# Token-order loads and DMA transposes for the last batch's q and k, in place of TensorE transposes

## The chip, the cores and the metric

The kernel runs on one core of one Trainium2 chip. The metric is the time of one execution on the device in microseconds (us). Most executions of a kernel agree within 0.3%. A profile's span is 1.7 to 2.1 us shorter than that time, so spans are compared with spans and times with times.

## The reference, cut to what matters

There are 4 batches, 8 heads, 768 tokens, head size 64, 512 channels. Attention uses a local window of 96 tokens and 8 global tokens with a distance bias. Its output goes through a gated mixing over tokens and then a matmul over channels.

```python
scores = scale * np.matmul(q, k.transpose(0, 1, 3, 2))      # + bias, mask, softmax -> a
x = np.matmul(a, v)                                         # heads side by side: 768 x 512
theta = x @ w_theta
zr, zi = x * np.cos(theta), x * np.sin(theta)
y = np.einsum('ts,bsd->btd', w_tok_r, zr) + np.einsum('ts,bsd->btd', w_tok_i, zi)
u = x + y
out = u + np.maximum(u @ w_ch, 0.0)
```

q and k are drawn with a factor of 0.1, so the scores are small beside the bias. The comparison with the reference doesn't see q and k well.

## The kernel before

While batch b is mixed, batch b+1 goes through attention, and q and k of batch b+2 are transposed for it (`prep`). So a "mixing stage" holds three kinds of work. The stage is the mixing of batch 1, with attention of batch 2 and, before the change, `prep` of batch 3.

```python
def load_qk(b, h0, n, which=(0, 1)):          # GpSimd DMA, 6 tokens x 64 = one run per head and partition
    ...
        nc.gpsimd.dma_start(out=qk[:, i_, h0:h0 + n]..., in_=(q, k)[i_][b, h0:h0 + n].rearrange("h (p t) d -> p h (t d)", p=T))

def prep(b, p):                               # one pair of heads
    ...                                       # VectorE: qkn <- qk, two copies
    for i_, dst in ((0, qT), (1, kT)):
        ps = ps_small([T, NT, T], BF)
        with behind("pe"):
            for t_ in range(NT):
                nc.tensor.transpose(ps[:, t_, :], qkn[:, t_, i_].rearrange("p h d -> p (h d)"), ident)
        ...
        if i_ == 0: nc.vector.tensor_copy(out=dst, in_=src)      # qT
        else:       nc.scalar.copy(out=dst, in_=src)             # kT
    kglob(b, p)

def kglob(b, p):                              # VectorE: kG <- kT, then the global tokens' columns over it
    ...
    nc.vector.tensor_copy(out=kG, in_=kT[:, T:(NT - 1) * T].rearrange("p (t n) -> p t n", t=NT - 2))
    nc.vector.tensor_copy(out=kG[:, :, 0:NG], in_=kT[:, None, 0:NG].to_broadcast([T, NT - 2, NG]))

def xtrans(b, p, ...):                        # xT <- x_sb, needed by theta
    if b: nc.sync.dma_start_transpose(...)
def utrans(b, tt):                            # uT <- u, needed by the channel matmul
    ...   nc.sync.dma_start_transpose(out=uT, in_=u)

def mix(b, tt, g): ...                        # TensorE: ps <- zri, w_tokT; then VectorE: u <- x_sb, ps

def load_behind(b, tile):                     # called for batch 3, once theta of batch 1 can start
    g = nc.gpsimd.tensor_copy(out=gate, in_=tile).ins
    with tc.issue_after(g):
        load_all_qk(b)
        load_all_v(b)
```

Outside a few hand-ordered parts, a scheduler decides in which order each engine's queue holds the instructions. `behind("pe")` and the like name an instruction that must come first in that queue. The whole kernel:

The softmax here doesn't subtract the row's maximum and nothing guards it: scores larger than these inputs give would overflow.

## Time and profile before

The time is 176.44 us (median of 3 runs, 176.21 to 176.53).

| what | value | view |
|---|---|---|
| TensorE busy | 92% of a span of 174.7 us | page, part 1 |
| chain of waits: TensorE, VectorE, DMA | 56%, 23%, 4% | page, part 4 |
| TensorE busy in the altered stage, 76 to 108 us | 31.3 of 32 us | stretches |
| xT by DMA, 66 to 130 us: issue to landing, median and longest | 2.8 and 7.3 us | tile view |
| batch 3's loads: issued; last (v) landed | 73.7 to 78.3 us; 96.1 us | GpSimd timeline, tile view |

From the page of before, parts 1, 2 (a digit is the busy share of a fortieth of the span, in tenths) and 4:

```profile
PE 160.6 (92%) x1505; PEld 86.4 (49%) x1530; DVE 133.9 (77%) x300; ACT 102.2 (58%) x128; POOL 26.3 (15%) x31
PE   6469878999999899999999999999999989999991
PE 56%; DVE 23%; ACT 13%; DMA 4%; issue 2%; DVEq 0%; ACTq 0%
```

TensorE (PE) is at 8 or 9 tenths in every slice from the seventh to the last but one.

The stretch table of before, a row for each 4 us of the stage (start:end, length, busy time and instructions of each engine, granted TensorE clock, DMA, GB/s):

```profile
core 0: us, PE busy (x) PEld busy (x) DVE busy (x) ACT busy (x) POOL busy (x), PEclk, DMA share, GB/s
80.00:84.00 4.00, 3.88 (x36) 1.80 (x36) 2.10 (x5) 3.72 (x5) 0.00 (x0) 1.00 1.23 220
84.00:88.00 4.00, 3.73 (x52) 2.09 (x53) 3.49 (x7) 3.38 (x4) 0.00 (x0) 1.00 1.46 243
...
100.00:104.00 4.00, 3.95 (x47) 2.51 (x46) 3.93 (x9) 0.87 (x2) 0.00 (x0) 1.00 0.58 140
...
108.00:112.00 4.00, 3.95 (x19) 1.81 (x19) 2.93 (x8) 1.70 (x2) 0.00 (x0) 1.00 0.34 95
```

There is next to no idle TensorE time here. (The DMA share can exceed 1; it serves only to compare stretches.)

The chain of waits of before at the end of the stage (start, duration, what). L233 are the transposes that the change removes, L388 the mixing, L368 the theta matmuls with which batch 2's own mixing stage begins. Of their first 16, six can run before the last xT has landed, ten need it (the trace has a record of nine):

```profile
104.39 0.67 PE ps L233 x12
105.06 0.88 PE ps L413 x4
105.95 0.87 PE ps L233 x12
106.81 1.73 PE ps L388 x8
108.54 1.29 PE pb L368 x6
...
109.89 2.11 PE pb L368 x9
```

Twelve transposes cost 0.67 to 0.87 us of TensorE and lie on the chain. Theta of batch 2 gives two marks: its first matmul (108.38 us in TensorE's timeline) and the first that needs the last xT (109.89).

VectorE (DVE) in before, at the start of the stage:

```profile
77.42 1.91 DVE L377 TENSOR_TENSOR zri<-x_sb,cs 128x512 bf16<-128x512 bf16 x5
79.24 0.68 DVE L419 SCALAR_TENSOR_TENSOR o_sb<-ps,u 128x512 f32<-128x512 f32 x1
79.84 1.09 DVE L377 TENSOR_TENSOR zri<-x_sb,cs 128x512 bf16<-128x512 bf16 x3
```

The last three zri products, which every token tile of the mixing needs, are done by 80.9 us, and nothing stands in front of them.

### The profile page before, as it was taken

How to read it: one execution, taken by the hardware profiler on the slowest of the kernel's cores; microseconds unless marked ns; L12 is line 12 of the kernel's file. 1: busy time of each engine (PE TensorE's matmuls, PEld its weight loads, DVE VectorE, ACT ScalarE, POOL GpSimd, SP SyncE). 2: the span in 40 equal slices, each digit the busy share in tenths (PEclk: the TensorE clock that was granted, in tenths of full speed). 3: DMA queues.
4: the chain of work that ended last, by engine and by line, in shares of the span. 5: the costliest groups of instructions: out<-in, count | busy, mean ns of one | idle time of the engine just before them, and what ended most of it. 6: DMA issues, size and time to landing. Idle time of an engine off the chain costs nothing.

```text
span 174.7 us, 3707 instructions
## 1 busy us (share of the span) xinstructions
PE 160.6 (92%) x1505; PEld 86.4 (49%) x1530; DVE 133.9 (77%) x300; ACT 102.2 (58%) x128; POOL 26.3 (15%) x31
## 2 busy tenths in 40 slices
PE   6469878999999899999999999999999989999991
PEld 1245555456746566544455565443554634444440
DVE  7678965778999999996779999796866847723443
ACT  2479676999497694499854813779447408500010
POOL 8983355004000000190000000000000000000000
PEclk9999999999999999999999999999999999999999
DMA  5999999999999972479999955133145371414335
GB/s 157 183 192 182 206 208 208 204 205 165 166 204 167 159 116 45 109 90 216 244 148 103 168 135 135 34 121 90 21 87 134 90 168 27 172 31 101 114 90 180
DMA packets 58225, 24.36 MB, mean 139 GB/s; under 512 B 44256, under 2 KB 55264, under 8 KB 58208
## 3 DMA queue, kind: packets, MB, share of 16 engines
q0 software_dynamic: 35216, 12.45, 70.5%
q1 hardware_dynamic: 22576, 11.15, 28.8%
q10 hardware_dynamic: 416, 0.52, 0.9%
q8 instruction: 12, 0.20, 0.5%
q14 instruction: 5, 0.04, 0.1%
HBM read 25.69 MB, written 6.29 MB: 183 GB/s over the span
## 4 chain that ended last, share of the span: by engine, by line
PE 56%; DVE 23%; ACT 13%; DMA 4%; issue 2%; DVEq 0%; ACTq 0%
PE ps L388 25%; PE ps L413 10%; PE pb L368 7%; DVE x_sb L341 4%; PE pb L274 4%; PE pb L331 3%; ACT e L281 3%; PE ps L368 3%; ACT etab L133 3%; ACT cs L374 3%; DVE qT L238 2%; DVE e L291 2%; DMA qk<-in_k_dram 2%; DVE kG L208 2%; PE ps L233 2%
## 5 line engine op out<-in xcount | busy, mean ns | idle before, releaser
L388 PE MATMUL ps<-zri,w_tokT 128*128 128x512 bf16 x271 | 67.6, 379 | 1.2 <-issue 0.5
L281 ACT ACTIVATE e<-pb 128x1024 bf16<-128x1024 f32 (+1 forms) x48 | 43.5, 958 | 21.1 <-PE pb L274 21.0
L388 PEld LDWEIGHTS <-w_tokT 128*128 128x128 bf16 x288 | 25.9, 98 | 27.6 <-DVE w_tokT L160 0.6
L393 DVE TENSOR_TENSOR u<-x_sb,ps 128x512 bf16<-128x512 bf16 x24 | 16.4, 682 | 14.0 <-PE ps L388 14.0
L413 PE MATMUL ps<-w_ch_bf,uT 128*128 128x512 bf16 x94 | 23.7, 379 | 0.3 <-DVE u L393 0.2
L377 DVE TENSOR_TENSOR zri<-x_sb,cs 128x512 bf16<-128x512 bf16 x48 | 17.9, 418 | 7.9 <-ACT cs L374 7.6
L419 DVE SCALAR_TENSOR_TENSOR o_sb<-ps,u 128x512 f32<-128x512 f32 (+1 forms) x25 | 16.5, 662 | 3.1 <-PE ps L413 3.1
L274 PE MATMUL pb<-qT,kT 64*128 64x128 bf16 x224 | 15.6, 219 | 1.4 <-DVE qT L202 0.3
L291 DVE TENSOR_TENSOR e<-e,etab 128x1024 bf16<-128x1024 bf16 (+1 forms) x24 | 14.7, 616 | 2.5 <-ACT e L281 2.5
L274 PEld LDWEIGHTS <-kT 64*128 64x128 bf16 x224 | 9.1, 94 | 14.5 <-issue 12.5
L374 ACT ACTIVATE cs<-pb,halfpi 128x1024 bf16<-128x1024 f32 x8 | 8.9, 1115 | 11.5 <-PE pb L368 11.5
L240 ACT COPY kT<-ps 128x768 bf16<-128x768 bf16 x12 | 9.6, 798 | 10.3 <-PE ps L233 10.3
L368 PE MATMUL pb<-w_theta_bf,xT 128*128 128x512 bf16 x62 | 14.9, 379 | 0.6 <-DMA xT<-x_sb 0.5
L407 ACT COPY uT<-ps 128x512 bf16<-128x512 bf16 x7 | 4.1, 587 | 18.6 <-PE ps L406 18.6
L368 PEld LDWEIGHTS <-xT 128*128 128x128 bf16 x96 | 9.2, 98 | 11.1 <-DMA xT<-x_sb 1.0
L331 PEld LDWEIGHTS <-e 128*128 128x128 bf16 x352 | 12.6, 97 | 3.3 <-issue 1.6
L413 PEld LDWEIGHTS <-uT 128*128 128x128 bf16 x96 | 8.9, 98 | 10.0 <-ACT uT L407 0.3
L274 PE MATMUL pb<-qT,kG 64*128 64x128 bf16 x128 | 11.7, 217 | 1.5 <-DVE kG L209 1.4
L341 DVE TENSOR_TENSOR x_sb<-pb,rec 128x768 bf16<-128x768 f32 x12 | 11.4, 948 | 0.2
L79 POOL DMA_DIRECT2D vn<-in_v_dram x5 | 9.6, 1912 | 12.2 <-DVE vn L68 10.6
L238 DVE COPY qT<-ps 128x768 bf16<-128x768 bf16 x12 | 11.4, 947 | 0.0
L233 PEld LDWEIGHTS <-qkn 128*128 128x128 bf16 x144 | 9.0, 97 | 4.4 <-DVE qkn L218 1.4
(72 smaller groups left out, 200.9 us busy)
## 6 DMA issues: line engine op xcount, KB each, us to landing
out_dram<-o_sb SPq DMA_DIRECT2D x23, 256.0 KB, 2.2
qk<-in_q_dram POOLq DMA_DIRECT2D x3, 768.0 KB, 17.4
qk<-in_k_dram POOLq DMA_DIRECT2D x3, 768.0 KB, 19.3
vn<-in_v_dram POOLq DMA_DIRECT2D x3, 768.0 KB, 22.0
w_nat<-in_moe_w_tok_r_dram POOLq DMA_DIRECT2D x3, 384.0 KB, 14.0
w_nat<-in_moe_w_tok_i_dram POOLq DMA_DIRECT2D x3, 384.0 KB, 15.2
vn<-in_v_dram POOLq DMA_DIRECT2D x2, 384.0 KB, 8.8
qk<-in_q_dram POOLq DMA_DIRECT2D x3, 192.0 KB, 6.7
```

Source lines behind the costliest of these rows:

```text
L238: nc.vector.tensor_copy(out=dst, in_=src)
L274: nc.tensor.matmul(pb[:, hh, o:o + T], lhsT=lhsT, rhs=qT[R, (own, nxt)[part]], start=bool(b), stop=bool(b) or (jt == NT - 1 or (j == 1 and ...
L281: ins = nc.scalar.activation(e_c, pb[:, :, 0:n], AF.Exp, scale=scale).ins
L291: nc.vector.tensor_mul(e_c, e_c, tab[:, :, s0:s0 + n // T].rearrange("p a s n -> p a (s n)"))
L331: nc.tensor.matmul(o, lhsT=l_, rhs=r_, start=(i_ == 0), stop=(i_ == len(mms) - 1))
L341: nc.vector.tensor_mul(xv, po4[:, :, :, 0:D], rec.to_broadcast([T, n, NT, D]))
L368: nc.tensor.matmul(pb[j_] if last else pb[:, j_, :], lhsT=xT[:, dc, st(j_)], rhs=w_theta_bf[:, dc, :], start=(dc == 0), stop=(dc == NC - 1))
L377: nc.vector.tensor_mul(zri[b][:, i_, 2 * c + j_, :].rearrange("p (g d) -> p g d", g=NP), xb[:, :, 2 * c + j_, :], cs[:, i_, j_].rearrange( ...
L388: anchor["pe"] = nc.tensor.matmul(ps, lhsT=w_tokT[wi][:, st, tt * T:(tt + 1) * T], rhs=zri[b][:, wi, st, :], start=(st == 0 and wi == 0), ...
L393: anchor["dve"] = nc.vector.tensor_add(u_sb[b, tt].rearrange("p (g d) -> p g d", g=NP), x_sb[b][:, :, tt, :], ps.rearrange("p (g d) -> p g ...
L413: nc.tensor.matmul(ps_c, lhsT=uT[:, dc, :], rhs=w_ch_bf[:, dc, :], start=(dc == 0), stop=(dc == NC - 1))
L419: nc.vector.scalar_tensor_tensor(o_sb[:, cols], in0=ps_c[:, cols], scalar=0.0, in1=u[:, cols], op0=ALU.max, op1=ALU.add)
```

## The change

The intent is to relieve TensorE, the bounding engine. q and k of batch 3 are loaded in token order, one DMA per head and tensor (16 of them, with rows of 256 B), straight into the layout that a DMA transpose can take. SyncE issues eight DMA transposes to make qT and kT: pairs 0 and 1 in the mixing of batch 1, pairs 2 and 3 at the boundary to the next stage. That removes 48 transposes from TensorE, 8 qkn and 4 qT copies from VectorE, and 4 kT copies from ScalarE.

```diff
+    def load_qk_tokens(b):
+        qk = loads[b][0]
+        for h in range(H):
+            for i_ in range(2):
+                pair = qk[:, i_, h // 2 * 2:h // 2 * 2 + 2].rearrange("p h t d -> p (h t d)")
+                nc.gpsimd.dma_start(
+                    out=pair.rearrange("p (t h d) -> p t h d", t=NT, h=2)[:, :, h % 2],
+                    in_=(q, k)[i_][b, h].rearrange("(t p) d -> p t d", p=T))
...
+    def prep_dma(b, p):
+        qk = loads[b][0]
+        qkT[(b, p)] = [None, None, None]
+        for i_ in (1, 0):
+            to = qkT[(b, p)][i_] = att.tile([T, S], BF, name=("qT", "kT")[i_], bufs=6)
+            nc.sync.dma_start_transpose(
+                out=to.rearrange("p (t s) -> p t s", t=NT),
+                in_=qk[:, i_, 2 * p:2 * p + 2].rearrange("p h t d -> p (h t d)"))
...
         with tc.issue_after(g):
-            load_all_qk(b)
+            alloc_qk(b)
+            load_qk_tokens(b)
             load_all_v(b)
...
+        if b == B - 1:
+            add(0, kglob, b, 0)
...
+            if b == B - 1 and i_ in (0, 2, 6):
+                add(0, kglob, b, (1, 2, 0, 3)[i_ // 2])
...
-        ahead = [lambda p=p: prep(b + 2, p) for p in range(NP)] if b + 2 < B else []
+        ahead = [[lambda p=p: prep(2, p) for p in range(NP)], [lambda p=p: prep_dma(3, p) for p in range(2)],
+                 [], []][b]
         order = th[:4] + rest[:2] + th[4:] + rest[2:] if b else []
+        if b == 2:
+            order[:0] = [lambda p=p: prep_dma(3, p) for p in range(2, NP)]
```

The text of the change puts two pairs at the boundary and the kG copies in the next stage. The order that the scheduler built does neither: all eight transposes and all eight kG copies of batch 3 stand in SyncE's and VectorE's queues within the mixing of batch 1.

## The prediction

> **What bounds it now.** TensorE. The page has it busy 92% of 174.7 us. The chain of waits is 56% TensorE, led by the mixing matmuls (25%). In the stage that the change alters (mixing of batch 1 with attention of batch 2, about 73 to 109 us) the stretch table has TensorE busy 1.83 to 2.00 of every 2 us; VectorE is nearly as full from 94 to 109.
>
> **Removed.** 48 TensorE transposes: in the chain a group of 12 covers 0.67 us (one 0.87), so about 2.9 us of TensorE, all in that stage, nearly all critical. VectorE loses 8 qkn copies (0.34 us) and 4 qT copies (0.95), 6.5 us; ScalarE 4 kT copies (0.80), 3.2 us. If nothing else happened: 173.6 us.
>
> **Added.** 16 token-order loads of 768 rows of 256 B in place of 2. GpSimd issue took 0.72 us at 256 rows, 0.88 at 1024: about 0.85 each, 14 us, from 73.7 to 88. Movement: in the DMA stretches qk rows went at about 204 GB/s written, v (256 B rows) at about 155. The Trainium skill, "DMA: Bandwidth & Descriptors", Specifications, puts line rate at 512 B and up (this trace agrees). q and k then need 10 us rather than 7.7: issue paces them. v should land near 98 us, before its use at 109. Eight DMA transposes in SyncE's queue cost 1.2 us of issue and 2.8 us to landing (as the xT ones; 7.3 in contention).
>
> **Moved, and this costs.** In the built order the scheduler puts all eight kG copies of batch 3 early in VectorE's queue: the first ahead of the last three zri products of batch 1, the second pair before the first u. They wait for DMA-made kT. The same page (Anatomy of one DMA) says the issuing sequencer holds a semaphore wait: SyncE's eight transposes stand in order with outputs and uT.
> Estimate: the fourth load is issued near 77 and lands near 80; qT then kT of pair 0 issue at 79.5 and 80.7; kT lands 83.5 to 84.5. VectorE reaches that kG at 79.3: 4 to 5 us idle. The zri products held back finish at 86; TensorE's mixing of token tile 0 needs them at 82.5: a stall of about 3.5 us, where there was next to none. Pair 1's kG (kT about 87) delays VectorE a little; e products reach values(2,0) at about 90 against 87. Later kG break even. uT of batch 1 goes out at 88 rather than 84, needed at about 96: no stall.
>
> **Sum.** -2.9 + 3.5 + about 0.3 of secondary waits: +0.9 us. Predicted 177.3 us, range 174.6 to 181.0. Faster by over 2%: 0.05; within 2%: 0.78; slower by over 2%: 0.17.
>
> **What would show it.** Waits: a new line of VectorE kG waiting for DMA kT, longest 4 to 5 us, at 79 to 84; TensorE mixing waiting for zri, 3 to 4 us, at 82 to 86. From 90 us on TensorE without long gaps, theta of batch 2 starting at 108 to 110. GpSimd issues of 0.8 to 1.0 us. The stages after it unchanged within 0.5 us.
>
> **What would make it wrong.** kT of pair 0 landing by 81 (loads landing within 2.5 us): no stall, about 174. Or loads at 1.2 us of issue each and transposes slowed to 5 to 7 us by the load traffic: stalls at each of the four kG waits, uT late, 180 or more.

## The result, and the profile after

| kernel | median, us | lowest to highest | runs |
|---|---|---|---|
| before | 176.49 | 176.21 to 177.92 | 4 |
| after | 192.82 | 192.63 to 192.99 | 4 |

The ratio is 1.0907 (95% interval 1.0847 to 1.0967): the change makes the kernel 9% slower. A ratio here is the mean time of one kernel's runs over that of the other's of the same rounds, so it is not quite the ratio of the medians. Executions over 1.5% slower than the fastest of the same kernel are left out of the means. The prediction, 177.3 us and at most 181.0, was wrong.

From the page of after, parts 1, 2 and 4:

```profile
PE 165.8 (87%) x1457; PEld 86.0 (45%) x1482; DVE 128.4 (67%) x288; ACT 99.4 (52%) x124; POOL 38.0 (20%) x45
PE   5889979999999999923966669999999998999992
PEclk9999999999999999985578979999999999999999
DMA 32%; PE 32%; DVE 20%; POOL 8%; issue 3%; ACT 2%; SPq 1%; DVEq 0%; POOLq 0%
```

TensorE lost 48 instructions and yet is busy 5.2 us longer. There is a hole in its row at slices 18 to 24, which is 81 to 115 us, and in the same place the granted clock falls, to half at the lowest. The chain of waits, which DMA led for 4%, is now 32% DMA. Outside that stretch the row looks as before.

The stretch table of after:

```profile
80.00:84.00 4.00, 2.48 (x25) 1.08 (x24) 0.00 (x0) 3.37 (x4) 4.00 (x6) 1.00 2.24 126
84.00:88.00 4.00, 0.00 (x0) 0.00 (x0) 0.50 (x2) 0.00 (x0) 3.11 (x4) 0.57 2.05 175
...
100.00:104.00 4.00, 2.74 (x16) 0.93 (x14) 2.44 (x6) 1.02 (x1) 0.00 (x0) 0.80 2.01 136
...
108.00:112.00 4.00, 0.95 (x17) 0.51 (x17) 3.93 (x9) 1.03 (x2) 0.00 (x0) 0.98 0.46 91
```

From 84 to 88 us TensorE, ScalarE and almost all of VectorE stand still. Only GpSimd works: it issues loads. DMA is busier than in before, for longer.

VectorE's timeline of after. The bracket gives the idle time before an instruction and what ended it; L217 is the kG copy, L395 the zri products:

```profile
77.09 1.96 DVE L395 TENSOR_TENSOR zri<-x_sb,cs 128x512 bf16<-128x512 bf16 x5
87.50 0.29 DVE L217 COPY kG<-kT 128x512 bf16<-128x512 bf16 x1 [8.45 <-DMA kT<-qk]
...
88.31 1.08 DVE L395 TENSOR_TENSOR zri<-x_sb,cs 128x512 bf16<-128x512 bf16 x3
...
94.91 0.29 DVE L217 COPY kG<-kT 128x512 bf16<-128x512 bf16 x1 [4.63 <-DMA kT<-qk]
...
101.50 0.29 DVE L217 COPY kG<-kT 128x512 bf16<-128x512 bf16 x1 [3.23 <-DMA kT<-qk]
...
107.85 0.29 DVE L217 COPY kG<-kT 128x512 bf16<-128x512 bf16 x1 [3.06 <-DMA kT<-qk]
```

All four kG copies wait, not the first alone. The three zri products that ran at 79.84 us in before now run at 88.31, behind the first kG.

The waits of after, 70 to 145 us (engine and line, what for: us in total, times, longest), then the landing line of the kT transposes:

```profile
DVE kG L217 <- DMA kT<-qk: 19.4, 4, 8.4
PE ps L406 <- DVE zri L395: 6.6, 1, 6.6
```

```profile
DMA to landing us min/median/max: 7.2/8.8/9.9
```

Four pieces of the chain of waits of after:

```profile
79.67 6.45 DMA qk<-in_k_dram
...
86.26 8.62 DMA kT<-qk
...
98.75 9.07 DMA kT<-qk
...
125.90 2.33 PE pb L386 x10
```

The two kT transposes on the chain take 8.62 and 9.07 us from issue to landing. Ahead of the first stands the load of k of pair 1, itself 6.45 us from issue to landing. Theta of batch 2 starts at 124.08 us, 15.7 later than in before, waits 0.37 us for the last xT, and goes on at 125.90, 16.0 later. That is nearly all of the loss (the spans differ by 191.0 - 174.7 = 16.3 us).

The two in-order queues also held each other. From SyncE's timeline of after:

```profile
91.49 1.27 SPq L259 DMA_TRANSPOSE kT<-qk  x1
96.03 1.19 SPq L420 DMA_TRANSPOSE uT<-u  x1
...
98.75 3.48 SPq L259 DMA_TRANSPOSE kT<-qk  x1
```

uT could go out only at 96.03, because its u stood behind the second kG in VectorE's queue (94.91) and so behind the second kT. The fourth kT stood behind that uT in SyncE's queue; its load had landed by 96.1. It was issued at 98.75, and the fourth kG waited for it.

**The clock.** The span grew by 16.3 us; TensorE's busy time grew by 5.2 of it, its idle time by 11.1. Of the 5.2 us, 2.0 lie before 76 us, mostly at the kernel's start, where the change does nothing. From 76 us to the start of theta of batch 2 busy time grew by 2.9 us (34.7 against 31.8) and idle time by 12.6. Since about 2.9 us of transposes went from there, the same work took about 5.8 us longer (an estimate: 2.9 + 2.9). The group of mixing matmuls, over the whole span, shows most of it:

```profile
L388 PE MATMUL ps<-zri,w_tokT 128*128 128x512 bf16 x271 | 67.6, 379 | 1.2 <-issue 0.5
```

```profile
L406 PE MATMUL ps<-zri,w_tokT 128*128 128x512 bf16 x271 | 72.2, 401 | 8.1 <-DVE zri L395 6.6
```

The first line is of before, the second of after: the same number of matmuls (271 records in both), 4.6 us more. One-microsecond stretches of after show when the clock changes:

```profile
84.00:85.00 1.00, 0.00 (x0) 0.00 (x0) 0.00 (x0) 0.00 (x0) 1.00 (x2) 0.77 1.61 176
94.00:95.00 1.00, 1.00 (x5) 0.18 (x5) 0.10 (x1) 1.00 (x2) 0.00 (x0) 0.61 0.97 229
111.00:112.00 1.00, 0.66 (x10) 0.40 (x11) 1.00 (x3) 0.23 (x1) 0.00 (x0) 0.92 0.47 94
115.00:116.00 1.00, 1.00 (x5) 0.27 (x3) 0.69 (x1) 0.00 (x0) 0.00 (x0) 0.87 0.00 0
```

A mean of 0.77 in a stretch that starts at 1.0 and ends at 0.5 puts the change at 84.54 us. In the same way the others come to 94.78 (up), 111.84 (down) and 115.26 (up). The distances are 10.24, 17.06 and 3.42 us. (Between the second and the third there is one more dip, from 98.2 to 101.6 us, also 3.4 long.) The Trainium skill, "TensorE: Matmul & The Clock Gate", Part 1, says that the gate judges a free-running window of 3413 ns and halves the clock after an idle one. This trace agrees closely on the length: the distances are 3, 5 and 1 times 3.413. It does not bear out that the window has to be idle (see the end). In its windows at half clock TensorE is busy for 11.95 us in all, so half of that, 6.0 us, is an estimate of what the clock cost, close to the 5.8 above. So an idle gap here could cost twice, in itself and in half-speed work after it, and the second cost came in units of 3.4 us.

### The profile page after: what moved, and what is told of

Same layout as the page of the kernel before. It is cut to its first block, busy times and chain, and to the rows that moved or that the text cites. A ratio compares the mean times of both kernels' runs of the same rounds, so it can differ in the third digit from the quotient of the medians.

```text
span 191.0 us, 3630 instructions
## 1 busy us (share of the span) xinstructions
PE 165.8 (87%) x1457; PEld 86.0 (45%) x1482; DVE 128.4 (67%) x288; ACT 99.4 (52%) x124; POOL 38.0 (20%) x45
## 4 chain that ended last, share of the span: by engine, by line
DMA 32%; PE 32%; DVE 20%; POOL 8%; issue 3%; ACT 2%; SPq 1%; DVEq 0%; POOLq 0%
PE ps L406 18%; DMA qk<-in_k_dram 14%; DMA kT<-qk 9%; DMA w_nat<-in_moe_w_tok_r_dram 7%; PE ps L431 6%; DVE qT L247 4%; POOL qk L82 3%; DMA xT<-x_sb 3%; DVE e L309 3%; PE pb L386 2%; DVE x_sb L359 2%; PE pb L349 2%; POOL qk L73 2%; DVE qkn L227 2%; PE pb L292 2%
## 5 line engine op out<-in xcount | busy, mean ns | idle before, releaser
L406 PE MATMUL ps<-zri,w_tokT 128*128 128x512 bf16 x271 | 72.2, 401 | 8.1 <-DVE zri L395 6.6
L406 PEld LDWEIGHTS <-w_tokT 128*128 128x128 bf16 x288 | 27.2, 102 | 38.7 <-issue 13.4
L395 DVE TENSOR_TENSOR zri<-x_sb,cs 128x512 bf16<-128x512 bf16 x48 | 17.9, 418 | 8.5 <-ACT cs L392 8.1
L292 PE MATMUL pb<-qT,kT 64*128 64x128 bf16 x224 | 16.7, 228 | 5.5 <-DVE x_sb L359 4.6
L217 DVE COPY kG<-kT 128x512 bf16<-128x512 bf16 x16 | 5.0, 314 | 20.0 <-DMA kT<-qk 19.4
L392 ACT ACTIVATE cs<-pb,halfpi 128x1024 bf16<-128x1024 f32 x8 | 8.9, 1115 | 15.7 <-PE pb L386 15.7
L292 PE MATMUL pb<-qT,kG 64*128 64x128 bf16 x128 | 12.4, 225 | 0.2 <-DVE kG L218 0.2
L88 POOL DMA_DIRECT2D vn<-in_v_dram x5 | 9.6, 1919 | 12.6 <-DVE vn L68 10.2
L349 PE MATMUL pb<-vn,e 128*128 128x65 bf16 x168 | 9.9, 193 | 1.4 <-DVE e L309 1.0
L312 DVE TENSOR_TENSOR e<-e,etab 128x1024 bf16<-128x1024 bf16 x12 | 8.2, 684 | 3.5 <-ACT e L299 3.5
```

The costliest lines, as they stand in the source:

```text
L88: nc.gpsimd.dma_start(out=vn[:, h0:h0 + n, :, 0:D].rearrange("p h t d -> p (h t) d"), in_=v[b, h0:h0 + n].rearrange("h (t p) d -> p (h t) ...
L292: nc.tensor.matmul(pb[:, hh, o:o + T], lhsT=lhsT, rhs=qT[R, (own, nxt)[part]], start=bool(b), stop=bool(b) or (jt == NT - 1 or (j == 1 and ...
L349: nc.tensor.matmul(o, lhsT=l_, rhs=r_, start=(i_ == 0), stop=(i_ == len(mms) - 1))
L395: nc.vector.tensor_mul(zri[b][:, i_, 2 * c + j_, :].rearrange("p (g d) -> p g d", g=NP), xb[:, :, 2 * c + j_, :], cs[:, i_, j_].rearrange( ...
L406: anchor["pe"] = nc.tensor.matmul(ps, lhsT=w_tokT[wi][:, st, tt * T:(tt + 1) * T], rhs=zri[b][:, wi, st, :], start=(st == 0 and wi == 0), ...
```

## The experiments

Medians are beside the median of before in the same rounds. "Before" had 176.4 to 176.7 us in all of them. In the quoted expectations, theory A says that the waits of the kG copies in VectorE's queue are the loss, and its rivals say that the loss sits in the DMA traffic or in SyncE's order. Edits are against the changed kernel unless said otherwise.

| run | what | median, us | ratio to before (95%) |
|---|---|---|---|
| after | the change | 192.82 | 1.0907 (1.0847 to 1.0967) |
| e1 | kG copies late in VectorE's queue | 187.11 | 1.061 (1.0565 to 1.0656) |
| e2 | e1, 8 loads with rows of 1536 B (wrong) | 184.81 | one run |
| e3 | token-order loads, TensorE transposes | 177.93 | 1.0075 (1.0042 to 1.0108) |
| e4 | e1, DMA transposes behind uT in SyncE's queue | 182.65 | 1.0339 (1.0303 to 1.0375) |
| e6 | e4, all pairs at the boundary, kG on GpSimd | 176.14 | 1.0011 (0.9951 to 1.0072) |
| e7 | the change, loads issued at 35.7 to 70.0 us | 183.07 | 1.0358 (1.0317 to 1.0398) |
| e8 | e7 and e6 together | 182.40 | 1.0347 (1.0316 to 1.0379) |
| e9 | e6, v of batch 3 later, in halves | 177.21 | 1.0055 (1.0016 to 1.0095) |
| e10 | the change without its 16 loads (wrong) | 175.54 | 0.9953 (0.9925 to 0.998) |
| e11 | e6 without the 16 loads (wrong) | 175.33 | 0.9935 (0.9914 to 0.9957) |
| e12 | e6 for pairs 2 and 3 alone | 177.13 | 1.0039 (1.0017 to 1.006) |

### e1: the kG copies behind the mixing of batch 1

```diff
-        nc.vector.tensor_copy(out=kG, in_=kT[:, T:(NT - 1) * T]...)
+        with behind("dve") if b == B - 1 else nullcontext():      # behind the last u of batch 1
+            nc.vector.tensor_copy(out=kG, in_=kT[:, T:(NT - 1) * T]...)
```

> Only the eight kG copies of batch 3 move in VectorE's queue, from early in the mixing of batch 1 to behind the last u of batch 1; SyncE's order is unchanged. Theory A (the whole loss is VectorE held in order by kG copies waiting for kT): the 19.4 us of kG waits go, TensorE's 6.6 us wait for zri goes, about 174 to 175 us. Theory B (transposes and loads share the DMA engines, and SyncE's queue holds uT and xT behind eight transposes that wait for loads): the kG waits go, but chan of batch 1 now waits for uT, first uT landing near 100 us when TensorE wants it near 93; 180 to 185 us. Theory C (the loads alone slow everything): 188 or more.

It took 187.11 us (186.71 to 187.87), 5.7 less than the change. The waits of VectorE for kT are gone, and two others have come in their place. The waits of e1:

```profile
PEld L432 <- DMA uT<-u: 11.2, 2, 8.5
DVE o_sb L438 <- PE ps L432: 13.7, 8, 8.6
```

The channel matmul waits for uT. SyncE issues uT of the first token tile at 93.36 us (84.18 in before), because five of the transposes, issued from 79.41 to 91.02 us, stand in front of it in SyncE's queue; then it needs 7.74 us to land. So the kG waits were 5.7 us of a loss of 16.3, and theory A falls as the whole cause.

### e2: fewer and longer rows

```diff
-        for h in range(H):
-            for i_ in range(2):
-                ...                                   # 768 rows of 256 B
+        for p in range(NP):
+            load_qk(b, 2 * p, 2)                      # rows of 1536 B, one pair of heads
```

On top of e1. The tokens come out in another order, which is wrong.

> As e1_kg_late, but the 16 loads of 256 B rows are replaced by 8 loads of one pair each in rows of 1536 B: same bytes, a sixth of the packets; the result is wrong on purpose, because the tokens come in another order. If the 256 B packets are what slows the transposes (theory B1), kT and qT land 3 to 5 us after their issue in place of 6.0 to 9.9, and the time falls by 3 us or more against e1_kg_late. If any load traffic does it, or the transposes' own 768 packets (theory B2), they still take 6 us or more and the time is within 2 us of e1_kg_late.

One run took 184.81 us, 2.3 less than e1, between what the two sides expected. The landing line of kT tells more than the time does:

```profile
DMA to landing us min/median/max: 5.6/10.1/10.9
```

With rows of q and k six times as long the transposes land no sooner than in e1 (7.3, 8.4 and 9.4 us). Short rows of q and k are not needed for the slow landing. Whether short rows matter at all stays open: v, with rows of 256 B, was issued at 79.86 us and landed 24.2 us later, so it was in flight beside all eight transposes. The uT wait stays too, at 9.0 us.

### e3: the loads alone

```diff
+    def prep_tok(b, p):                               # as prep, but from the token-order tile: no qkn copies
+        ...
+                    nc.tensor.transpose(ps[:, t_, :], src[:, t_ * T:(t_ + 1) * T], ident)
...
-        ahead = [..., [lambda p=p: prep_dma(3, p) for p in range(2)], [], []][b]
+        ahead = [..., [lambda p=p: prep_tok(3, p) for p in range(NP)], [], []][b]
```

> Token-order loads kept, the DMA transposes undone: TensorE transposes straight from the loaded tiles (no qkn copies), at the places of the kernel before. If the transposes and their place in the queues make the loss, 175 to 177.5 us. If the 12288 small packets of the loads alone make it (theory C), 182 or more, with uT landing at 8 us or more.

It took 177.93 us (three runs from 177.83 to 178.00; a fourth, of 181.1, is a slow one and left out of the ratio): 1.4 us over before, a little above what was expected. Single uT and xT transposes took up to 10.2 and 10.6 us to land, at medians of 2.9 and 3.0. The loads without the DMA transposes of q and k therefore cost little, but the 2.7 us of VectorE's qkn copies that this version saves (8 of 0.34 us) don't show in the time either.

### e4: the transposes behind uT in SyncE's queue

```diff
+            with behind("sp"):                        # behind the last uT of batch 1 issued so far
                 nc.sync.dma_start_transpose(out=to..., in_=qk[:, i_, 2 * p:2 * p + 2]...)
...
-            nc.sync.dma_start_transpose(out=uT, in_=u)
+            anchor["sp"] = nc.sync.dma_start_transpose(out=uT, in_=u).ins
```

On top of e1.

> As e1_kg_late, and the eight DMA transposes are put in SyncE's queue behind the uT transposes traced before them, so that none of them waits for a load with uT behind it. Theory A: same as e1_kg_late. Theory B: uT of batch 1 lands in time as in the kernel before, no long TensorE gap in the mixing, 173 to 175.5 us: the 2.9 us of TensorE transposes are then saved.

It took 182.65 us (182.00 to 182.95), 4.5 less than e1 and far more than expected. Two pieces of its chain of waits:

```profile
90.56 9.00 DMA uT<-u
...
110.62 2.80 DMA xT<-x_sb
```

The first uT is now issued in time, at 83.93 us, and its matmuls run no later than in before. The second, in the lines above, lands 9.00 us after its issue: it is itself a DMA transpose and meets the same loads; TensorE waits 1.55 us for it. The last two xT are issued late, at 107.96 and 110.62 us, behind the transposes of q and k; theta of batch 2 waits 3.48 and 1.37 us for them. Moving the transposes in SyncE's order was worth 4.5 us, and what TensorE still waits for is DMA.

### e6: all pairs at the boundary, kG on GpSimd

```diff
# against e4
-        with behind("dve") if b == B - 1 else nullcontext(): ...
+        eng = nc.gpsimd if b == B - 1 else nc.vector
+        eng.tensor_copy(out=kG, ...)
...
-        ahead = [..., [lambda p=p: prep_dma(3, p) for p in range(2)], [], []][b]
+        ahead = [..., [], [], []][b]
-            order[:0] = [lambda p=p: prep_dma(3, p) for p in range(2, NP)]
+            order[:0] = [lambda p=p: prep_dma(3, p) for p in range(NP)]
```

> All eight DMA transposes of batch 3 stand in SyncE's queue behind the last uT of batch 1, so after the loads have landed (about 106 us) and after every xT and uT of the mixing; the kG copies of batch 3 run on GpSimd, idle by then, so neither VectorE nor SyncE holds anything behind a load. Theory B (place in the queues and the transposes' sharing of the DMA engines with the loads make the loss): kT and qT land in about 3 us each, uT and xT no slower than in e3_loads_only, 174 to 175.5 us, that is e3_loads_only less the 2.9 us of TensorE transposes. If DMA transposes cost as such (theory D: they slow whatever runs beside them), the loss moves to theta and attention of the next batch and the time stays at 178 or more.

It took 176.14 us, 176.39 for before: the same. Three runs lie between 176.08 and 176.18; the fourth, the profiled one, took 178.31. The transposes of q and k now land in 2.8 us (median of kT; longest 4.5), after the loads. The mixing of batch 1 ends earlier: its last eight matmuls start at 103.25 us, against 106.65 in before, 3.4 us sooner. Then, in the chain of waits of the profiled run:

```profile
101.51 6.27 DMA xT<-x_sb
...
107.83 4.92 PE pb L388 x14
```

The last xT but one takes 6.27 us to land, while v of batch 3 is still under way (it lands 18.4 us after issue, near 106). Theta of batch 2 starts at 104.98 us but could continue only at 107.83, after 2.25 us of idle TensorE, and in this run then at half clock. In this run the gain of 3.4 us was turned into a wait for a transpose that the change doesn't even touch. The other three runs are 2.2 us faster, two of them with a granted clock of 1.000 throughout, so they can't have lost all of this; they have no trace that shows how much of the wait they share.

### e7 and e8: loading early

```diff
-    def load_qk_tokens(b): ...                        # into the qk buffer, at 73 us
+    def load_qk_tokens(b, p):
+        pairs[p] = moe.tile([T, 2, S], BF, name="w_nat", bufs=6)      # a buffer whose weights are used up
...
+                if b == 0 and g == 1 and tt in (0, 2):                # in the mixing of batch 0
+                    main.append((0, lambda tt=tt: [load_qk_tokens(3, tt + p) for p in range(2)]))
```

e7 is the change with this edit; e8 has e6's edits too.

> The change's own queue orders, left to the scheduler, but the token-order loads are taken off the critical time: they go to the four w_nat buffers that are dead by then, two pairs from about 45 us, two from about 57 us, so that no kT waits for a load. Only v is still loaded behind the gate. Theory B: the kG waits shrink from 19.4 us to under 5, kT and qT land in 3 to 5 us for want of load traffic, 174.5 to 178 us. If the order in SyncE's queue alone is at fault, uT still waits and it stays at 182 or more; if the transposes are slow in themselves, kT still takes 7 us or more to land.

> Both: early loads as in e7_early_load, transposes at the boundary and kG on GpSimd as in e6_boundary. Theory B: no contention in the mixing of batch 1 and nothing held in order, so the saving of the TensorE transposes shows: 173 to 174.5 us. Theory D: 177 or more.

They took 183.07 and 182.40 us: about 10 better than the change, and 6 to 7 worse than before. The loss moved upstream. The landing line of xT of batch 1, 60 to 80 us, in e7:

```profile
DMA to landing us min/median/max: 7.7/8.2/8.2
```

In before these same xT landed in 2.7 to 3.9 us. In e7 theta of batch 1 starts at 71.55 us, as in before (71.87), but waits for xT twice; the ten matmuls that need the last xT start only at 78.0 us and at half clock (3.98 us), where before had them done by 75.5. The transposes of q and k themselves do land sooner than in the change (kT median 3.5 us, longest 8.2). The theories here asked where the loads do no harm; neither place is free of harm.

### e9: v later

```diff
# against e6
-            load_all_v(b)
+    def load_v_behind(b, tile):                       # tile: kT of batch 3, pair 0
+        ...
+            load_v(b, 0, 4)
+            load_v(b, 4, 4)
```

> As e6_boundary, but v of batch 3, whose load was in flight until 106 us and beside which xT took 6.3 us to land, is loaded in two halves after kT of pair 0 has landed (about 110 us), and its vG copies are moved to match. Theory B: xT of batch 2 lands in about 3 us, theta of batch 2 starts near 105.5 us in place of 107.8 and at full clock; 173.5 to 175 us if v lands in time for the values of pair 0 (wanted near 121 us), up to 176.5 if it is late. If the v traffic was not the cause, no change from e6_boundary (176.1).

It took 177.21 us (176.53 to 178.15), 0.5 more than before (176.71). Theta of batch 2 starts at 104.84 us, waits 0.51 us for the last xT, and goes on at 106.80 at full clock, 3.1 earlier than in before, so moving v away did free xT. (The edit also fixes the order of the kG copies on GpSimd and moves the vG copies.) Then the chain has:

```profile
112.09 12.87 DMA vn<-in_v_dram
...
125.03 4.25 DMA uT<-u
```

The gain was given back one stage later: v now lands too late, and the transposes of q and k that it overlaps take up to 10.5 us, with no load of q or k in flight.

### e10 and e11: no q/k loads at all

```diff
-            alloc_qk(b)
-            load_qk_tokens(b)
+            loads[b] = [loads[b - 1][0], None]        # batch 2's q and k stand in for batch 3's
             load_all_v(b)
```

Wrong on purpose: the transposes and the kG copies are all there and as early in their queues, but nothing is loaded for them. (The scheduler's order around them is not the same in every place.) e10 is the change with this edit, e11 is e6 with it (and the order of the kG copies on GpSimd fixed).

> The change with the 16 token-order loads left out: the DMA transposes read batch 2's q and k instead (wrong result on purpose), v is still loaded; VectorE's kG copies and SyncE's transposes stay as early and as interleaved as the scheduler puts them. Theory B (load traffic makes the transposes slow and the in-order queues only pass it on): kT and qT land in 3 to 5 us, kG waits under 3 us in all, 173.5 to 176 us. If the queue orders are a fault of their own even without loads: 178 or more.

> e6_boundary with the same instruction order on TensorE, VectorE, ScalarE and SyncE, but without the 16 loads (wrong result on purpose). It is what the change could give with no load traffic of its own. If the 2.9 us of TensorE transposes were all critical: 173.3 to 173.8 us. If they also covered the landing of the last xT of batch 2 (theory E: part of the removed work was filler), xT of pair 3 is waited for by 1 us or more at theta and it stays at 174 to 175 us.

e10 took 175.54 us (before 176.71). The change with its early places for kG and the transposes, which took 192.82, is a little faster than before once its 16 loads are gone: 17.3 us less. With e3 this makes a square: loads without the DMA transposes cost 1.4 us, DMA transposes without the loads cost nothing, both together 16.3. The loss is in their meeting. The landing line of kT in e10:

```profile
DMA to landing us min/median/max: 2.8/3.4/5.0
```

Of the four kG waits one is left, of 2.3 us, and TensorE stays busy for 3.16 of 4 us around it. This edit takes away the loads' traffic and their issuing on GpSimd, and the wait of a transpose for its own load. Landing times count from the issue of the transpose, when its load is already there, so the fall of the median from 8.8 to 3.4 us is not that wait: it goes with the traffic (or its issuing). The transposes also go out earlier (the first at 72.35 us), and v, issued at 75.41, lands in 13.1 us. The kT issued beside v alone (at 84.63) took 5.0.

e11 took 175.33 us, slightly above what the more hopeful side expected. Its mixing of batch 1 ends 3.3 us early, as in e6, but the last mixing stage starts at 147.90 us against 149.96, and its end is 1.4 us earlier in time (175.33 against 176.71). So 1.2 us of the 3.3 are lost by then, 0.5 of it in a wait of theta of batch 2 for xT. The other 0.7 us go after the last matmul, where the last output lands in 2.9 us against 2.2. The cause of that last difference is not known. So even with no load of q and k to disturb it, this change is worth 0.65%, not the 1.6% of 2.9 us.

### e12: half of the change

```diff
# against e6
     def load_qk_tokens(b):
-        for h in range(H):
+        load_qk(b, 0, 4)                              # pairs 0 and 1 as before
+        for h in range(4, H):
...
-        ahead = [..., [], [], []][b]
+        ahead = [..., [lambda p=p: prep(3, p) for p in range(2)], [], []][b]
-            order[:0] = [lambda p=p: prep_dma(3, p) for p in range(NP)]
+            order[:0] = [lambda p=p: prep_dma(3, p) for p in range(2, NP)]
```

> A version that might beat both: only pairs 2 and 3 of batch 3 are loaded in token order and transposed by DMA, at the boundary as in e6_boundary with kG on GpSimd; pairs 0 and 1 keep the row loads and TensorE transposes of the kernel before. It saves 24 TensorE transposes (about 1.4 us) and adds half of the small-row traffic (8 loads), so that v should land near 100 us in place of 106 and the last two xT of batch 2 in 3 to 4 us. Theory B: 175.0 to 176.0 us, faster than the kernel before by 0.3 to 0.8%. If the traffic still delays xT or uT at the boundary: 176.2 or more.

It took 177.13 us over 6 runs, 176.49 for before over 11: 0.4% slower, a real difference (1.0017 to 1.006). v lands in 13.9 us, sooner than in before, and the wait of theta of batch 2 for xT is down to 0.18 us. Theta starts at 106.92 us and goes on with the last xT at 108.57, 1.5 and 1.3 us earlier than in before: the halved saving is there. It is lost in the next stage: SyncE issues the last xT of batch 3 at 140.72 us, against 140.63 in before. What takes it there was not followed further.

No correct version was found that beats the kernel before; e6 equals it.

## Why the prediction was wrong, point by point

**The bound, and the saving: right.** TensorE was the bound. The 2.9 us that the removed transposes should save is there: in e6 and e11 the mixing ends 3.4 and 3.3 us earlier. (Both also lack VectorE's and ScalarE's copies, and their kG is on GpSimd.) That the saving reaches the end in full was assumed, and e11 shows 1.4.

**The loads' issue: right.** GpSimd's 16 issues took 0.82 to 0.94 us each but for the first, until 87.2 us (predicted 0.85 and 88). Pair 0 was there on time: its transposes were issued at 78.86 and 80.24 us (predicted 79.5 and 80.7).

**The order of the queues: right, though not all that follows from it.** The first kG stood in front of three zri products, TensorE waited for zri, and uT waited behind the transposes in SyncE's queue. The Trainium skill, "DMA: Bandwidth & Descriptors", Anatomy of one DMA, says that a DMA's semaphore wait is held by the issuing sequencer; e1's SyncE agrees: uT went out at 93.36 us, though its u was done by 84.0. What the prediction lacked is that the two queues would hold each other, so that one late kT delays the issue of a later one.

**The landing time: wrong, and this is the step that failed.** The prediction wrote "2.8 us to landing (as the xT ones; 7.3 in contention)" and then had kT of pair 0 land at "83.5 to 84.5", that is 2.8 to 3.8 us after its issue. It took 7.2, and the four kT had a median of 8.8 us. The 2.8 is the median of the xT, of which those with no load beside them took 2.7 to 2.8. These eight transposes run just behind 16 loads and beside the load of v. The loads had the same fault: the prediction had the fourth land about 3 us after its issue, and that held (at most 3.4); but k of pair 1, the eighth, took 6.45 us, and later ones up to 10.2. So the transposes of pair 1 could go out only at 84.73 and 86.26 us. The trace of before had the right number in it: the first uT of batch 1 and the first xT of batch 2, the ones beside batch 3's loads, took 7.8 and 7.3 us.

What followed from that term:
- The first kG wait was 8.4 us, not "4 to 5", and TensorE's wait for zri 6.6 us, not 3.5.
- "Later kG break even" was false: the waits were 4.6, 3.2 and 3.1 us. In none of the places that the scheduler chose was a transpose of 9 us done when its consumer came.
- "uT of batch 1 goes out at 88 ... no stall": it went out at 96.03.
- The clock was not in the sum at all. It was halved for 10.2, 3.4 and 3.4 us in a stage with gaps of up to 6.6 us, which stretched the work by about 6 us (the estimate above).
- v landed at 107.7 us, not 98.

The prediction named this branch ("transposes slowed to 5 to 7 us by the load traffic: stalls at each of the four kG waits, uT late, 180 or more"), though it tied it to loads of 1.2 us of issue each, which did not come. It gave the branch too little weight (0.17 for slower by over 2%), and had the landing too small.

**Where the 16.3 us lie.** A ladder of runs with more undone at each step:

| step | us | what it removes |
|---|---|---|
| after to e1 | 5.7 | kG waits passed on by VectorE's queue |
| e1 to e4 | 4.5 | uT held in SyncE's queue behind waiting transposes |
| e4 to e6 | 6.5 | the transposes of q and k beside the loads, ahead of xT; kG moved to GpSimd |
| e6 to before | -0.4 | the rest, with the saved 2.9 us in it |

The last row is 176.49 - 176.14, with its sign turned. And e10 takes one root away for all of them: without the loads, with the early places of the transposes and the kG copies kept, the loss is gone. So it is shown that the in-order queues pass the loss on (e1, e4), and that it needs the loads (e10) and the DMA transposes beside them (e3). The shares of the ladder depend on the order of the steps.

**What stays open.** Why a transpose lands three times as late beside these loads is not settled. The Trainium skill, "DMA: Bandwidth & Descriptors", Issuing engines are not separate DMA queues, says that DMAs from all engines run on the same 16 DMA engines and interleave, and its section Queues, rings and completion order says that an engine takes turns between queue rows packet by packet. That fits e9, where kT takes 9.5 and 10.5 us beside v alone, and e10. But then longer rows and fewer loads might have changed it, and e2 shows no faster landing (there v's short rows stayed). Which load does it is not settled either: in the change the first kT (7.2 us) landed before v was issued, while the fourth (9.1) was issued after the last load of q and k had landed and met v alone of the loads; beside v alone in e10 kT took only 5.0. Sharing is argued here, not shown; that the slow landing and the loss go when the 16 loads go is shown.

## What to carry to other kernels

Cost a DMA at the landing time that the trace shows for the moment where it will run, beside the loads that run then, and not at its median: here it was 8.8 us against 2.8. Moving work from a full engine to DMA is only free where the consumer comes later than that, and where nothing that matters stands behind the consumer, or the issue, in an in-order queue. If TensorE is the bound, look in the trace for half-speed time after new gaps, and add it: here it was about 6 us. (It set in 2.1 us into one gap and after a string of gaps of at most 0.81 us, but not after one gap of 1.5 us, so these runs give no rule by length.)

## What the Trainium skill lacked or had wrong

- "DMA: Bandwidth & Descriptors", DMA Transpose (X-bar) and the rules: no figure for a transpose's landing time beside ordinary loads. The rules say that a transpose next to ordinary DMAs "needs nothing", which is about correctness; the time went from 2.8 us (e6, after the loads) to 7.2 to 9.9 us (the change).
- The same page, Specifications: it puts line rate at 512 B and up. Loads with 256 B rows did move more slowly (v at about 155 GB/s against 204 for q and k, in before), but longer rows of q and k did not help a transpose beside them (e2, median 10.1 us, with v's short rows still there). The page says that DMAs interleave; it has no figure for how much a load delays others (here kT went from a median of 3.4 us in e10 to 8.8).
- The same page: no issue cost for many small loads from GpSimd. Here it was 0.82 to 0.94 us for 768 rows and 2.2 us for the v load, during which nothing else can be issued from it.
- The same page: no issue cost of a transpose on SyncE. Here it was 1.2 to 1.3 us when undisturbed and up to 3.5 us beside the loads.
- "TensorE: Matmul & The Clock Gate", Part 1: the 3413 ns free-running window agrees with this trace. Its table of the two states speaks of an idle window, but the windows that halved the clock were not wholly idle: the one that ended at 84.54 us had begun at 81.13 with 1.3 us of matmuls in it, so a gap of 2.1 us was enough. The one from 94.78 to 98.19 halved it with 2.09 us of TensorE busy and no gap over 0.81 us, while the one from 101.61 to 105.02, busy for 1.90 us, did not. So busy time alone doesn't decide, and the page gives no share that does. After that drop the clock stayed low for three windows (TensorE idle through the first and partly in the second), after the later ones for one.
- No page has the cost of the kG copy on GpSimd: 0.61 us, against 0.29 us on VectorE.
